# A layer's forward and backward in one kernel: split evictions, narrow tiles on demand, a sum over groups from two bf16 parts, a softmax gradient in halves

## The chip, the cores and the metric

One core of a Trainium2 chip runs the whole program. The time is that of one launch in device microseconds (us); lower is better. The engines are named as the profile names them: PE (matrix multiplication), PEld (its weight loads), DVE, ACT, POOL and SP. SP computes nothing here, it issues DMAs, and POOL and ACT can issue them too. Each engine runs its own list of instructions strictly in the order in which it was written.

## The reference

The program computes a layer's output and ten gradients. With `xn = layernorm(x)` (2048 tokens, 512 wide) the output is `x + A(xn) + B(xn)`.

A is attention with a recurrent memory, 32 heads of 128. The tokens are cut into 64 segments of 32. Segment `s` works on 40 rows: 8 memory rows and its own 32 tokens.

```
h = concat(mem, x_s)                       # 40 x 512
q, k, v = h Wq, h Wk, h Wv                 # 32 heads x 128
p = softmax(q k^T / sqrt(128) + mask);  o = (p v) Wo
mem, out_s = o[:8], o[8:]                  # mem goes to segment s+1
```

So segment `s+1` can't begin before `s` has given its memory: a chain of 64 steps forward, and in the backward pass a chain of 64 steps the other way, in which the gradient of the memory rows is handed from segment `s` to `s-1`. B is `relu(xn w1 + b1)^2 w2 + b2`, without a chain. In the code the eight rows of a segment that pass to the neighbour stand with its 24 other rows in the "A" tiles of 32 rows, and the remaining 8 rows of four segments are batched into "L" tiles of 32 rows, which are off the chain.

## The kernel before, in words

Four stages follow one another. (1) Layernorm and B, forward and backward. (2) The forward chain: 64 calls of `chain(s)`, with the batched work of 16 blocks of four segments (`l_proj`, `l_attn`, `blk_in`, `blk_out`) and two weight gradients of B (`dw_unit`, 14 units of 16 pairs of matmuls) as filler between the links. (3) The backward chain: another `chain(s)`, 64 steps, with `l_pre`, `l_post`, `load` and `blk_out`. (4) The weight gradients of A, dense 128x128 matmuls, with the gradient of the layernorm beside them.

In stages 1 to 3 the code does not issue instructions where it stands. Each piece of work is put into a `_Plan` as an operation with a cost for each engine that may run it, with the tiles that it reads and writes. `_Plan.run` then writes one order for all engines: it simulates them, ranks operations by the longest way to the end, adds a correction for each operation from the tables `BIAS_1` and `BIAS_2` and follows the parameters `PAR`. PSUM banks are handed out by the same planner (`Stage.bank`, with a limit for each kind). What the chip then does at its own pace keeps that order on every engine, so a late operand stops the engine that waits for it, and whatever stands behind.

PE runs three shapes of matmul: full tiles of 128x128 (plan form `f`: transposes, `blocks`, `dw_unit`), four column tiles of 128x32 side by side (`w`: `proj` at line 538, `dh_part` at L1370, `wo_part` at L1039, scores at L1161), and sixteen tiles of 32x32 of which the diagonal four are used (`d`: `diag` at L624, the second half of `mixed` at L599). Going from one shape to another is what the planner calls a turn. In the kernel before, each operation has one shape.

The forward step is `proj` of q and k (evicted by `evict`, 512 columns at once), transposes of both (`to_T`, L429), a mask matmul (L1153) and the scores into one PSUM bank (L1161), `weights` (row maximum L1007, subtraction L1008, exponential L1010), transposes of the weights on DVE (L1168, L1169), `diag` "o" (L624), whose result is scaled on eviction (L634 or L639), a DVE transpose (`sq_T`, L517), `wo_part` (L1039), and `mb` (L1046, L1047), from which matmul L1185 takes the memory rows that DVE copies (L1190) into the next segment's input `hA`. POOL normalises the weights for the backward pass (L1020, L1021).

The backward step is `proj` "gO" (L538), its transposes, `dP` into one PSUM bank (L1468), the softmax gradient `smax_bwd` (four DVE operations over all eight head groups, L1354 to L1359) giving `dS`, DVE transposes of it (L1501, L1502), and three parts 2, 1, 0 (gradients of v, q, k): each makes `dN` (L573, L588 with L599, L624), transposes it on DVE (L517) and multiplies with the weight into the bank `ps_dRA` (`dh_part`, L1370). Its sum `R_A` is evicted in float32 by two copies (ACT and DVE); 32 float32 matmuls with the selector `sel8` (L1524) sum it over the four groups of rows, and DVE copies the sum into `gT` of the next step (L1528), from which `proj` "gO" reads.

## Time and profile before

| | us |
|---|---|
| median of three runs | 2809.19 |
| lowest and highest run | 2799.02, 2809.37 |
| span of the profiled execution (first to last instruction) | 2798.3 |
| stage 1, from the start | 228 |
| stage 2, forward chain | 1007 |
| stage 3, backward chain | 1022 |
| stage 4, weight gradients | 542 |

No time of its own is given for the profiled execution beside its span. The stages are cut at the first matmul of the forward chain, the first of the backward chain, and where the weight gradients take over, so they overlap by a few us at the cuts. In the page, the busy time of PE counts from the start of a matmul to its modelled end, so that a single short matmul counts for its whole way through the array; how closely matmuls follow each other is better read from the starts in the timeline. A wait is named by the instruction that waited and the one that released it.

### The profile page before, as it was taken

How to read it: one execution, taken by the hardware profiler on the slowest of the kernel's cores; microseconds unless marked ns; L12 is line 12 of the kernel's file. 1: busy time of each engine (PE TensorE's matmuls, PEld its weight loads, DVE VectorE, ACT ScalarE, POOL GpSimd, SP SyncE). 2: the span in 40 equal slices, each digit the busy share in tenths (PEclk: the TensorE clock that was granted, in tenths of full speed). 3: DMA queues.
4: the chain of work that ended last, by engine and by line, in shares of the span. 5: the costliest groups of instructions: out<-in, count | busy, mean ns of one | idle time of the engine just before them, and what ended most of it. 6: DMA issues, size and time to landing. Idle time of an engine off the chain costs nothing.

```text
span 2798.3 us, 125071 instructions
## 1 busy us (share of the span) xinstructions
PE 2664.6 (95%) x54888; PEld 1538.5 (55%) x55072; DVE 1327.3 (47%) x3327; ACT 985.8 (35%) x2012; POOL 824.8 (29%) x2431
## 2 busy tenths in 40 slices
PE   8998999999999999999999999999999899999999
PEld 6664555555555555575555555555555444444444
DVE  5544455555455555565455455555455402232322
ACT  4333444444444444364444444444444300000000
POOL 1111111111111111145555555555555301112210
PEclk9999999999999999999999999999999999999999
DMA  6657656555557566647777676777766698788861
GB/s 211 202 172 205 180 160 175 164 166 163 156 169 186 169 185 175 177 118 178 187 181 187 179 189 179 189 192 190 188 182 177 201 344 273 232 255 270 257 185 42
DMA packets 499792, 530.91 MB, mean 190 GB/s; under 512 B 223845, under 2 KB 325398, under 8 KB 497070
## 3 DMA queue, kind: packets, MB, share of 16 engines
q1 hardware_dynamic: 480254, 463.06, 59.9%
q0 software_dynamic: 15056, 53.56, 5.6%
q8 instruction: 430, 7.05, 1.1%
q10 hardware_dynamic: 3936, 6.29, 0.7%
q14 instruction: 116, 0.95, 0.1%
HBM read 249.77 MB, written 237.52 MB: 174 GB/s over the span
## 4 chain that ended last, share of the span: by engine, by line
PE 45%; DVE 4%; issue 3%; DMA 3%; ACT 1%; POOL 1%; SPq 0%; DVEq 0%; ACTq 0%; POOLq 0%
PE ps_gw L1690 14%; PE ps_dRA L1370 8%; PE ps_gw L1694 5%; PE ps_gO L538 3%; PE ps_dRL L1370 3%; PE ps_d L624 2%; DMA dLN<-S_GNL 2%; PE ps_d L573 1%; PE ps_d L599 1%; PE ps_gOT L429 1%; PE ps_d L588 1%; PE ps_gm L1524 1%; PE ps_gL L538 1%; PE ps_dL L1481 1%; PE ps_dP L1468 1%
## 5 line engine op out<-in xcount | busy, mean ns | idle before, releaser
L1370 PE MATMUL ps_dRA<-WA,dT 128*32 128x512 bf16 x6144 | 377.0, 381 | 5.3 <-issue 2.5
L1690 PE MATMUL ps_gw<-WA,WB 128*128 128x512 bf16 x1505 | 330.6, 379 | 1.6
L1690 PEld LDWEIGHTS <-WB 128*128 128x128 bf16 x1896 | 185.4, 98 | 225.0 <-issue 1.7
L538 PEld LDWEIGHTS <-PA 128*32 128x32 bf16 x8192 | 195.4, 96 | 192.3 <-DVE PA L1190 22.3
L435 ACT CAST dN<-ps_d 128x512 bf16<-128x512 f32 x372 | 207.4, 590 | 184.7 <-PE ps_d L599 112.3
L1370 PEld LDWEIGHTS <-dT 128*32 128x32 bf16 x6144 | 151.8, 96 | 154.2 <-DVE dT L517 17.3
L433 DVE CAST gwo<-ps_gw 128x512 bf16<-128x512 f32 x64 | 40.0, 685 | 399.9 <-PE ps_gw L1690 268.5
L435 ACT CAST gwo<-ps_gw 128x512 bf16<-128x512 f32 x64 | 33.1, 598 | 510.2 <-PE ps_gw L1690 357.3
L517 DVE STREAM_TRANSPOSE dT<-dN 128x256 f32<-128x256 f32 x384 | 165.4, 437 | 72.1 <-ACT dN L435 66.5
L1020 POOL TENSOR_TENSOR P<-P,rsA 128x320 bf16<-128x320 bf16 x64 | 46.2, 722 | 458.8 <-DVE rsA L1015 244.1
L624 PEld LDWEIGHTS <-PB 32*32 32x32 bf16 x8192 | 119.8, 92 | 76.4 <-DVE PB L1168 23.9
L1701 POOL DMA_DIRECT2D out_dram<-gwo x96 | 71.6, 753 | 293.9 <-ACT gwo L435 265.1
L538 PE MATMUL ps_q<-WA,PA 128*32 128x512 bf16 x2048 | 145.2, 382 | 5.5 <-DVE PA L1190 3.7
L1039 PE MATMUL ps_RA<-WB,OT 128*32 128x256 bf16 x4096 | 129.0, 277 | 17.7 <-DVE OT L517 13.6
L538 PE MATMUL ps_k<-WA,PA 128*32 128x512 bf16 x2048 | 144.9, 381 | 0.3 <-DVE PA L1190 0.3
L435 ACT CAST kN<-ps_k 128x512 bf16<-128x512 f32 x125 | 73.4, 587 | 194.1 <-PE ps_k L538 172.2
L538 PE MATMUL ps_v<-WA,PA 128*32 128x512 bf16 x2048 | 140.7, 379 | 0.0
L1039 PEld LDWEIGHTS <-OT 128*32 128x32 bf16 x4096 | 103.9, 98 | 46.2 <-DVE OT L517 32.0
L538 PE MATMUL ps_gO<-WB,PA 128*32 128x512 bf16 x2048 | 126.4, 380 | 1.0 <-DVE PA L1528 1.0
L611 POOL COPY BDL<-bPLL 32x64 bf16<-32x64 bf16 x256 | 60.4, 236 | 218.4 <-PE ps_d L573 210.4
L433 DVE CAST qN<-ps_q 128x512 bf16<-128x512 f32 x62 | 42.9, 692 | 171.5 <-PE ps_q L538 169.5
L1254 PE MATMUL ps_dw<-sx,anT 128*128 128x512 bf16 x339 | 108.2, 384 | 6.6 <-DMA sx<-S_XN 2.8
(315 smaller groups left out, 5300.8 us busy)
## 6 DMA issues: line engine op xcount, KB each, us to landing
S_GN<-dN SPq DMA_DIRECT2D x192, 256.0 KB
WA<-S_GN SPq DMA_DIRECT2D x150, 256.0 KB
S_Q<-qN SPq DMA_DIRECT2D x64, 256.0 KB
S_K<-kN SPq DMA_DIRECT2D x64, 256.0 KB
S_V<-vN SPq DMA_DIRECT2D x64, 256.0 KB
S_ON<-oN SPq DMA_DIRECT2D x64, 256.0 KB
bqN<-S_Q SPq DMA_DIRECT2D x64, 256.0 KB
bkN<-S_K SPq DMA_DIRECT2D x64, 256.0 KB
```

The costliest lines, as they stand in the source:

```text
L433: nc.vector.tensor_copy(out, in_)
L435: nc.scalar.copy(out, in_)
L517: self.plan.add({"DVE": 0.445}, lambda e, half=half: nc.vector.transpose(words(dst, half).rearrange("p (i c r) -> p i c r", i=4, c=2), src ...
L538: nc.tensor.matmul(bk()[32 * j:32 * (j + 1), :], lhsT=win(dc), rhs=Wt(dc, c0), start=(dc == 0), stop=(dc == DC - 1), tile_position=(0, 32 ...
L611: f(q_(dst, j)[:, :, j, 0:c], q_(src_f(), j))
L624: nc.tensor.matmul(bk()[32 * j:32 * j + m, k * P:(k + 1) * P], lhsT=lf(j, i), rhs=rf(j, i), start=(k == 0 and x == 0), stop=(x == n - 1), ...
L1039: nc.tensor.matmul(bk()[32 * c:32 * (c + 1), :], lhsT=sg.rows(OTt, i, j), rhs=Wo[:, JQ * i + j, dh * DH:(dh + 1) * DH], start=(i == 0 and ...
L1254: nc.tensor.matmul(bks[x]()[:], lhsT=anT[x][:, c, :], rhs=sx[z][:], start=(c == 0), stop=(c == TC - 1))
L1370: nc.tensor.matmul(bk()[32 * j:32 * (j + 1), :], lhsT=sg.rows(XT, i, j), rhs=wtf(t, i, j), start=(first and i == 0), stop=(last and i == N ...
L1690: nc.tensor.matmul(bks[n](), lhsT=HNc[:, rc, dc * P:(dc + 1) * P], rhs=gns[y][:, hf * 512:(hf + 1) * 512], start=(y == 0), stop=(y == NRC ...
L1694: nc.tensor.matmul(bks[n](), lhsT=gns[y][:, k * P:(k + 1) * P], rhs=GOc[:, rc, :], start=(y == 0), stop=(y == NRC - 1))
L1701: nc.gpsimd.dma_start(outWs[t][dc * P:(dc + 1) * P, 4 * hf:4 * hf + 4, j, :], wt[:].rearrange("p (i e) -> p i e", i=4))
```

## The change

The edits lie in the planner and in stages 2 and 3; the work of stages 1 and 4 is as it was (two small mask tiles move into the pool of stage 1).

Planner: an operation can have two shapes (`"wf"`), and the planner takes the one that PE is in. A key can have parts. New costs, new `PAR`, and new tables `BIAS_1` and `BIAS_2` throughout, so that the order of both chains is a new one.

Forward: the evictions of q and k and of their transposes are cut in two (`evict2`); the scores lie in two banks of four head groups, and mask, maximum, subtraction, exponential and DVE transposes go by halves; the scaled eviction of "o" goes by quarters; `P40` has two buffers. `dw_unit` and the transposes off the chain may run as 128x32 tiles. The batched scores (and in the backward pass `dPL`) take one matmul with 64 columns where there were two with 32. `blk_out` moves only the 32 memory rows of a block, in both chains; the other rows of `S_HNA` and `S_GOA` are copied from DRAM to DRAM. These copies, the memory rows of K and V, and the rows for `dw_unit` (two blocks of rows to a DMA) are now issued by POOL instead of SP. The writer of the key `"tk"`, by which some copies were paced, is gone. The batched output rows go straight to the output, without `S_BL`, `S_OL` and the last copy.

Backward: `R_A` is read as two bf16 parts, its upper half words in place and `R_lo`, the rest, which DVE makes by a subtraction; 32 bf16 matmuls take the place of the 32 in float32. `dP` lies in two banks, and `smax_bwd` makes its four operations twice, on halves of four head groups.

```diff
-PAR = ((0.3, 0.3, 0.0), (0.61, 7.94, 4.04), (0.09, 2.05, 17.32))
+PAR = ((0.3, 0.3, 0.0), (0.0, 0.45, 38.57), (0.0, 0.41, 55.23))
...
-                turn = o.shape not in (None, shape)
+                turn = bool(o.shape) and shape not in o.shape
...
     def transpose_to(ps_ap, in_ap, base=0, form="f"):
         k = in_ap.shape[0]
+        if form == "w":
+            for c in range(4):
+                x = slice(32 * c, 32 * c + 32)
+                nc.tensor.transpose(ps_ap[x], in_ap[:, x], ident[:], tile_position=(0, 32 * c))
+            return
...
+    def copy_tokens(b, dst, src):
+        sg.dma(lambda: dst[b * P + RL:(b + 1) * P].rearrange("(r v) d -> r v d", v=SPB),
+               lambda: src[b * P:(b + 1) * P].rearrange("(v r) d -> r v d", r=SEG)[M:], [("tk", b * SPB - 2)], [], cost=0.7, eng="POOL")
...
+    SPLIT = ("q", "k")
+    SPLIT_T = ("qT", "kT")
...
+        def evict2(self, out_f, bk, in_f, key, prio, cost, n=2):
+            self.plan.parts[key] = [(key, x) for x in range(n)]
+            for x in range(n):
+                c = slice(512 // n * x, 512 // n * (x + 1))
+                self.plan.add(cost, lambda e, c=c: ev({"DVE": "v", "ACT": "s"}[e], out_f(c), in_f(c)), [bk], [(key, x)], prio)
...
         def to_T(self, kind, nm, src, skeys, out_f, okeys, prio):
+            form = "wf" if prio else "f"
...
-        sg = Stage(plan, pc, {"c": (5, F8), "f": (2, F8), "m": (2, F8), "t": (1, F8)})
+        sg = Stage(plan, pc, {"c": (6, F8), "f": (2, F8), "m": (2, F8), "t": (1, F8)})
...
+            for h in range(2):
+                x, bk = slice(4 * h, 4 * h + 4), bks[h]
+                A({"DVE": 0.325}, lambda e, x=x, bk=bk: V.tensor_reduce(mx[:, x], bk()[:], axis=AX.X, op=ALU.max), [bk], [("mxA", h)], 0)
+                A({"DVE": 0.325}, lambda e, x=x, bk=bk: V.tensor_tensor(
+                    out=st[:, x], in0=bk()[:], in1=mx[:, x].unsqueeze(2).to_broadcast([P, 4, KA]), op=ALU.subtract),
+                  [bk, ("mxA", h)], [("stA", h)], 0)
+                A({"ACT": 0.345}, lambda e, x=x: nc.scalar.activation(Et[:, x], st[:, x], ACT.Exp, scale=scale), [("stA", h)], [(pk, h)], 0)
...
             for nm, D_, S_ in (("S_V", S_VM, S_V), ("S_K", S_KM, S_K)):
                 sg.dma(lambda D_=D_: mrow(D_[b])[:, M * v:M * (v + 1), :], lambda S_=S_: mrow(S_[s])[:, 0:M, :],
-                       [(nm, s)], [(nm + "M", b, v)])
+                       [(nm, s)], [(nm + "M", b, v)], cost=0.7, eng="POOL")
...
-        sx = [tl("sx%d" % x, [P, D]) for x in range(5)]
+        sx = [tl("sx%d" % x, [P, 2, D]) for x in range(3)]
...
+                z = c // 2 % 3
+                if c % 2 == 0:
+                    sg.dma(lambda z=z: sx[z][:], lambda c=c: src[c * P:(c + 2) * P, :].rearrange("(c p) d -> p c d", p=P), [], [("sx", z)], lat=3.2, cost=0.62, eng="POOL")
 
                 def mm(e, c=c, z=z):
+                    w = 32 if e == "w" else P
                     for x in range(2):
-                        nc.tensor.matmul(bks[x]()[:], lhsT=anT[x][:, c, :], rhs=sx[z][:], start=(c == 0), stop=(c == TC - 1))
-                A(pe(0.435, "f", 2), mm, [("sx", z), ("anT", 0, c // HC), ("anT", 1, c // HC)], [bks[0], bks[1]])
+                        for m in range(0, P, w):
+                            nc.tensor.matmul(bks[x]()[m:m + w, :], lhsT=anT[x][:, c, m:m + w], rhs=sx[z][:, c % 2, :], start=(c == 0),
+                                             stop=(c == TC - 1), tile_position=(0, m))
+                A(pe(0.435, "wf", 2), mm, [("sx", z), ("anT", 0, c // HC), ("anT", 1, c // HC)], [bks[0], bks[1]])
...
+        R_hi = R_A.bitcast(BF16).rearrange("p (d z) -> p z d", z=2)[:, 1]
+        R_lo = tl("R_lo", [P, D])
+        sel8b = tl("sel8b", [P, M])
+        nc.vector.tensor_copy(sel8b[:], sel8[:])
...
+            for h in range(2 if sfx == "A" else 1):
+                x = slice(4 * h, 4 * h + 4) if sfx == "A" else slice(0, NI)
+                n = 4 if sfx == "A" else NI
+                c = cD if sfx == "L" else 0.315
...
                 for hf in range(2):
-                    def gm(e, hf=hf):
-                        for dc in (2 * hf, 2 * hf + 1):
-                            for j in range(JQ):
-                                nc.tensor.matmul(q_(bm(), j)[:, dc, :], lhsT=R_A[:, dc * P + 32 * j:dc * P + 32 * (j + 1)],
-                                                 rhs=sel8[:], start=(dc == 0), stop=True, tile_position=(0, 32 * j),
-                                                 skip_group_check=True)
-                    A(pe(0.31, "w", 16), gm, [("RA", hf)], [bm], 0)
+                    A({"DVE": 0.42}, lambda e, hf=hf: V.tensor_tensor(
+                        out=R_lo[:, 256 * hf:256 * hf + 256], in0=R_A[:, 256 * hf:256 * hf + 256], in1=R_hi[:, 256 * hf:256 * hf + 256],
+                        op=ALU.subtract), [("RA", hf)], [("Rl", hf)], 0)
+                for part_, key in ((R_hi, "RA"), (R_lo[:], "Rl")):
+                    for hf in range(2):
+                        def gm(e, hf=hf, part_=part_, key=key):
+                            for dc in (2 * hf, 2 * hf + 1):
+                                for j in range(JQ):
+                                    nc.tensor.matmul(q_(bm(), j)[:, dc, :], lhsT=part_[:, dc * P + 32 * j:dc * P + 32 * (j + 1)],
+                                                     rhs=sel8b[:], start=(dc == 0 and key == "RA"), stop=True, tile_position=(0, 32 * j),
+                                                     skip_group_check=True)
+                        A(pe(0.065, "w", 8), gm, [(key, hf)], [bm], 0)
...
-        sg.dma(lambda: seg_rows(out0flat, SEG, 0, M), lambda: seg_rows(S_OL, M, 0, M), [("gm", 0, SPB - 2)], [])
```

More of the change, by code (lines that the diff above doesn't have):

```diff
@@ L100, in pe @@
     x.shape = shape
-    x.n = n
+    x.n = {k: n * (4 if k == "w" and len(shape) > 1 else 1) for k in shape}
     return x
@@ L285, in run @@
                     elig.append(u)
-            seq.append((o, e))
+            seq.append((o, form if form and len(o.shape) > 1 else e))
         assert len(seq) == len(ops)
@@ L577, in blocks, with mixed @@
                            bk, lambda bk=bk: bk()[:], [(dst[0], half)], prio, EV_F)
-        def mixed(self, nm, pre, terms, rkeys, dst, prio, lift=0.0):
-            bks = [self.bank("d", [P, 512], F32, "ps_" + nm) for _ in range(2)]
-            for half in range(2):
+        def mixed(self, nm, pre, terms, rkeys, dst, prio, lift=0.0, full=False, inter=False, kind=None):
+            bks = [self.bank(kind or "d", [P, 512], F32, "ps_" + nm) for _ in range(2)]
+            for half in ((0, 1) if not inter else ()):
                 bk = bks[half]
@@ L699 @@
+        for i in range(NI):
+            nc.vector.tensor_copy(maskA[:, i, M:KA], mk[:])
         RB = 2 * P
@@ L1462, in chain @@
             sg.to_T_plain("c", "gOT", gN, "gN", gOT, "gOT", 0)
-            bk = sg.bank("c", [P, NI, KA], F32, "ps_dP")
+            bkp = [sg.bank("c", [P, NI // 2, KA], F32, "ps_dP") for _ in range(2)]
             for half in range(2):
```

361 lines of the change are left out of this document (194 added, 167 removed), and 55 rows, old and new, of tables (BIAS_1, BIAS_2).

## The prediction

> **What bounds the kernel now.** I read the totals first, then the stages, then what PE waited for in each chain, then single steps in order of time. The totals:
>
> ```profile
> span 2798.3 us, 125071 instructions
> PE 2664.6 (95%) x54888; PEld 1538.5 (55%) x55072; DVE 1327.3 (47%) x3327; ACT 985.8 (35%) x2012; POOL 824.8 (29%) x2431
> PEclk9999999999999999999999999999999999999999
> ```
>
> PE is busy for 95% of the span and the granted clock is full in all forty slices, so the time is the length of PE's list plus 134 us of gaps. The same by stage (columns: stretch, its length, then busy us and instructions of PE, PEld, DVE, ACT, POOL, then clock, DMA share, GB/s), with the rows that give the cuts:
>
> ```profile
> 228.00:1235.00 1007.00, 939.65 (x23959) 570.44 (x24066) 541.39 (x1316) 449.81 (x919) 154.95 (x294) 0.99 0.62 172
> 1235.00:2257.00 1022.00, 974.83 (x26969) 578.96 (x26969) 521.00 (x1291) 416.69 (x822) 540.22 (x1917) 1.00 0.72 186
> 2257.00:2799.00 542.00, 535.23 (x2442) 243.62 (x2490) 146.73 (x240) 33.15 (x64) 93.26 (x136) 1.00 0.73 228
> ...
> L538 PE MATMUL ps_q<-WA,PA x2048: 376/379/634, 228.5 to 1192.4; 128*32 128x512 bf16 x187
> ...
> L538 PE MATMUL ps_gO<-WB,PA x2048: 376/379/391, 1235.5 to 2211.5; 128*32 128x512 bf16 x187
> ...
> 2257.64 10.73 PE ps_gw L1690 x49
> ```
>
> The last stage, 542 us with 535 of PE, is dense and untouched; so is the first. What can move lies in the two chains: 67 us of PE gaps in the forward one, 47 in the backward one, and whatever a busy PE wastes. What PE waited for in the forward chain, then in the backward one (total, times, longest):
>
> ```profile
> PE ps_RA L1039 <- DVE OT L517: 13.6, 16, 2.0
> PE ps_o L624 <- DVE PB L1168: 10.2, 11, 4.1
> PE ps_mem L1185 <- DVE PB L1047: 7.4, 10, 1.1
> PE ps_q L538 <- DVE PA L1190: 3.7, 12, 0.3
> PE ps_dw L1254 <- DMA sx<-S_XN: 2.8, 4, 1.0
> ...
> PE ps_d L599 <- DVE maskA L1359: 3.4, 6, 1.2
> PE ps_gO L538 <- DVE PA L1528: 1.0, 3, 0.3
> ```
>
> The first four are links of the recurrence: 34.9 us in which the forward chain, not PE, set the pace. In the backward chain the link into the next step, `gO` on the copy L1528, costs 1.0 us in 63 steps: there PE has other work, and instructions removed from it count nearly in full.
>
> What a busy PE wastes shows in a forward step (start, duration; PE alone):
>
> ```profile
> 702.75 1.04 PE L1254 MATMUL ps_dw<-sx,anT 128*128 128x512 bf16 x3
> 703.86 0.22 PE L1185 MATMUL ps_mem<-sel,PB 128*32 128x16 bf16 x8
> 704.01 0.60 PE L1254 MATMUL ps_dw<-sx,anT 128*128 128x512 bf16 x2
> 704.55 0.61 PE L538 MATMUL ps_q<-WA,PA 128*32 128x512 bf16 x8
> ...
> 708.25 0.40 PE L429 MATMUL ps_qT<-ident,qN 128*128 128x128 bf16 x4
> ...
> 709.70 0.27 PE L1161 MATMUL ps_sc<-KT,qT 128*32 128x40 bf16 x16
> 709.81 0.60 PE L538 MATMUL ps_v<-WA,PA 128*32 128x512 bf16 x8
> ...
> 710.98 0.67 PE L1108 MATMUL ps_scL<-KT,qLT 128*32 128x32 bf16 x64
> 711.48 0.62 PE L538 MATMUL ps_v<-WA,PA 128*32 128x512 bf16 x8
> 712.03 0.39 PE L1254 MATMUL ps_dw<-sx,anT 128*128 128x512 bf16 x1
> 712.48 0.39 PE L429 MATMUL ps_hN<-ident,PA 128*128 128x128 bf16 x4
> 712.79 0.23 PE L624 MATMUL ps_o<-vN,PB 32*32 32x128 bf16 x4
> ```
>
> The 49 dense matmuls of 10.73 us above follow each other by 0.22 us. The two of `ps_dw` at 704.01 should so take 0.44 us, but the next shape starts 0.54 us after them: the turn costs 0.10. PE goes into full tiles four times in these ten us.
>
> And a backward step, around the hand-over and at a change of shape:
>
> ```profile
> 1560.62 0.37 ACT L435 COPY R_A<-ps_dRA 128x256 f32<-128x256 f32 x1 [2.98 <-issue]
> 1561.03 0.42 DVE L433 COPY R_A<-ps_dRA 128x256 f32<-128x256 f32 x1 [2.91 <-ACT R_A L435]
> 1561.23 0.59 PE L1524 MATMUL ps_gm<-sel,R_A 128*32 128x8 f32 x32
> 1561.75 0.23 PE L624 MATMUL ps_dqL<-bkLN,dSTLL 32*32 32x128 bf16 x4
> 1561.89 0.19 DVE L1528 CAST PA<-ps_gm 128x32 bf16<-128x32 f32 x1 [0.44 <-PE ps_gm L1524]
> 1562.31 1.91 PE L538 MATMUL ps_gO<-WB,PA 128*32 128x512 bf16 x32
> ...
> 1565.19 0.22 PE L573 MATMUL ps_d<-gON,BDP 128*128 128x128 bf16 x1
> 1565.25 0.22 PE L573 MATMUL ps_d<-gLN,BDL 128*128 128x128 bf16 x1
> 1565.40 0.23 PE L624 MATMUL ps_dqL<-bkLN,dSTLL 32*32 32x128 bf16 x4
> ```
>
> Full tiles of 128 columns follow by 0.06 us, and the next shape by 0.15: again 0.09 for the turn.
>
> **The sum, against the span of 2798.3 us.** The median of the three runs, 2809.19, lies 10.9 us above that span; I take the difference over.
>
> *Forward, turns.* With two shapes to choose from, `ps_dw` and `ps_hN` can stay in the narrow shape that PE is in. In the step shown the visits at 702.75 and 704.01 would each save two turns, that at 712.03 (between narrow and 32x32 tiles) one; the transposes of q and k at 708.25 keep theirs. Five turns of 0.10 us over 64 steps are 32 us; the low end is nothing, if the planner's new order does not use the choice. In narrow form the work of `ps_dw` itself is that of a projection, 8 matmuls in about 0.44 us (709.81 and its kind), so it is no dearer. Not each step holds as many visits: I take two thirds, -22.
>
> *Forward, waits.* The halves shorten the recurrence. A copy of 512 columns that becomes two of 256 on two engines:
>
> ```profile
> L435 ACT CAST dN<-ps_d 128x512 bf16<-128x512 f32 x372 | 207.4, 590 | 184.7 <-PE ps_d L599 112.3 <-PE ps_d L624 36.8 <-DVE gOT L433 9.8
> L1354 DVE TENSOR_TENSOR btA<-ps_dP,bP 128x320 f32<-128x320 f32 x64 | 31.3, 490 | 30.2 <-PE ps_dP L1468 29.3 <-DMA LT<-S_VM 0.6
> ```
>
> 0.59 us against 0.37 (the half copy of `R_A` on ACT): -0.2 at each of four places (q and k, their transposes, the scaled eviction, the start of the softmax on the first half of the scores), some 0.8 us a step. The turns take 0.34 us of cover from the same gaps (22/64), which leaves 0.46 against a mean wait of 34.9/64 = 0.55. Ends: none, and all 34.9; I take two thirds, -23. The extra instructions cost no time of their own while DVE and ACT are at 54% and 45% of the stage.
>
> *Small work on PE.* `ps_scL`, 64 matmuls in 0.50 us, becomes 32 twice as wide: between 0.25 and 0.50, so -0.2, 16 times; the same for `dPL`: -3 in each chain. The block transposes (712.48 to 712.79, less a turn: 0.2) become four narrow ones of 0.06: -0.15, 32 times, -2.5 in each chain.
>
> *Backward, the sum of R.* The 32 float32 matmuls take 0.52 us up to the next, 0.10 of it a turn. Sixteen narrow bf16 matmuls with 40 columns take 0.11 us (709.70 to 709.81), so 32 of them 0.22: -0.2 over 63 steps, -13. The strided read of the upper halves as weights has no row; if it doubled those 16, the gain would be -6, if the new ones cost as much as the old, 0. I take -13, by the nearest row. The page "TensorE: Matmul & The Clock Gate" of the Trainium skill, section "Back-to-back issue gap", speaks against this: it gives up to 64 columns a floor of some 60 cycles, 25 ns, for each matmul, by which 32 would take an estimated 0.8 us, +24 us instead of -13, and a sum of -24 instead of -61. The scores' row, 7 ns each over four column tiles, disagrees, so I leave that sum a place only within the second case below.
>
> *Backward, the link.* Before the lower part can be multiplied, DVE subtracts twice, each about as long as its copy of that width, 0.42. With ACT making both copies (done at 1560.99 and 1561.36), the subtractions end at 1561.83 and the copy L1528 starts near 2.05 instead of 1.89; with DVE making the second copy, near 2.5. So +0.15 to +0.6 us a step. In the step shown the copy ends 0.23 us before `gO` starts, because PE is on `ps_dqL`: that other work is the cover, and where it is used up the whole 0.15 to 0.6 counts, and the matmuls saved as well. Ends: 0 and 0.4 x 64 = 25; I take +8.
>
> *Backward, the halves of the softmax gradient.* From 0.42 at 256 columns and 0.49 at 320, 160 columns take 0.31: eight make 2.5 us where four made 2.0. The first half is done after 1.25, so part 1 can begin earlier; the DVE transposes of all `dS` come up to 0.5 later, less what the first `dP` bank is earlier. Ends: -5 (the wait at L599, 3.4, and some) and 0.2 x 64 = 13. I take 0, since what waits on `dS` now sums to a few us. DVE rises by some (0.5 + 0.84) x 64 = 86 us to 59% of the stage.
>
> *The moved DMAs.* Some 112 loads of `sx`, 128 copies of memory rows and 64 other copies go from SP to POOL. POOL's issues in this stage:
>
> ```profile
> L479 POOL DMA_DIRECT2D out_dram<-wt x28: 542/678/807, 319.6 to 1208.1; - x28
> ```
>
> At 0.68 us, 304 make 207 us, and POOL goes from 155 to 362 of 1007 us. I cost it at nothing while they are issued ahead of need; the price otherwise is the third case.
>
> Forward -22 - 23 - 5.5 = -50.5; backward -13 + 8 + 0 - 5.5 = -10.5; together -61. 2798.3 - 61 = 2737, and with 10.9: **2748 us**.
>
> **The rivals.** *The chains take it back* (0.24). The backward link costs its 25 and the halves their 13, against -18.5: +19.5, and with the forward gain -31, 2778. For it: PE's spare work shrinks in every step while the link grows. Against it: 1.0 us of waits there today.
>
> *Late loads from POOL, slower* (0.12). PE keeps its order, so each `sx` pair that lands late stops it in full. On POOL the load stands behind copies that must wait until K or V has landed in DRAM, and behind the normalisation L1020. Over 112 loads the break-even with -61 is 0.55 us each, and above 0.67 the kernel is slower by more than 0.5%; at 0.8 the time is 2809 - 61 + 90 = 2838. Against it: three buffers hold six blocks of rows where five were held, and today such waits are 2.8 us in all. The Trainium skill's "SBUF — State Buffer", section "Who interferes with whom", adds a reason: DVE in its two-port modes locks GpSimd out, descriptor generation with it. The spread of 542 to 807 ns in the row above agrees, but is at most 0.27 us an issue.
>
> *The change does not do what it says* (0.06). The new order seldom uses the second shape, and PE's saved work turns into waits: within 0.5%, about 2805.
>
> **How the numbers follow.** The sum has 0.58, with its own range 2700 to 2775: all turns and waits, and no cost of the link, give -32 - 35 - 11 - 13 = -91 and 2718, and an order that also closes other gaps some 20 less. About 0.5% (14 us) is what a measurement of this kernel tells from no change. Faster: 0.58 + 0.24 = 0.82; same 0.06; slower 0.12. The range 2690 to 2812 leaves out the late loads and about 0.05 below.
>
> **What would show it.** The forward stretch near 955 us and the backward near 1010; `ps_dw` largely as 128x32 tiles; the waits of `ps_RA`, `ps_o`, `ps_mem` and `ps_q` near 12 us together; `ps_gm` as 32 bf16 matmuls followed by the next within 0.3 us; the wait of `gO` on the copy of `ps_gm` under 10 us. I am wrong if PE waits on `sx` for tens of us, if `gO`'s wait grows past 20, or if the narrow form of `ps_dw` takes clearly more than 0.44 us a pair.

## The result, and the profile after

The changed kernel is slower. Its median is 2917.8 us of four runs (2912.8 to 2925.3) beside 2809.3 for the kernel before on the same chip: a ratio of 1.0395, 95% interval 1.0368 to 1.0422, some 108 us where I had forecast a gain of 61. The totals of the page, to be read against those of before:

```profile
span 2911.0 us, 130411 instructions
PE 2685.9 (92%) x56746; PEld 1544.9 (53%) x56746; DVE 1448.6 (50%) x4455; ACT 1001.0 (34%) x2287; POOL 1044.5 (36%) x2764
```

PE's busy time rose by 21 us and its gaps from 134 to 225. (More busy time isn't more work here: with the halves alone, below, nearly the same number of matmuls counts 15 us more.) By stage, cut at the first matmul of `ps_q`, the first of `ps_gO` and the start of the dense `ps_gw` (columns as in the prediction: stretch, length, busy us and instructions of PE, PEld, DVE, ACT, POOL, then clock, DMA share, GB/s):

```profile
231.00:1319.60 1088.60, 961.96 (x25910) 583.98 (x25906) 606.97 (x1996) 487.32 (x1250) 350.30 (x611) 0.98 0.61 160
1319.60:2360.60 1041.00, 959.05 (x26721) 566.59 (x26714) 575.88 (x1728) 392.12 (x759) 564.12 (x1932) 0.98 0.70 178
2360.60:2911.00 550.40, 546.94 (x2533) 247.73 (x2532) 146.66 (x240) 33.15 (x64) 93.83 (x137) 1.00 0.76 230
```

By the same cuts the chains of the kernel before take 1007.0 and 1012.4 us, so the forward chain lost 82 us and the backward chain 29. (The same forward chain takes 1089 to 1101 us in three profiles, of this kernel and of two runs that edit only the backward chain, so some 12 us in a single profile are chance.) In the forward chain PE's gaps went from 67 to 127 us. What PE waited for, in the forward chain and then in the backward one:

```profile
PE ps_RA L1089 <- DVE OT L536: 25.5, 48, 1.5
PE ps_o L669 <- issue: 12.2, 9, 3.1
PE ps_vL L563 <- POOL PB L1111: 11.1, 1, 11.1
PE ps_mem L1238 <- DVE PB L1097: 9.0, 18, 1.0
PE ps_kT L435 <- DVE kN L439: 8.9, 5, 3.8
...
PE ps_dP L1536 <- DVE gOT L439: 36.9, 13, 6.5
PE ps_d L643 <- DVE maskA L1429: 11.6, 25, 0.8
```

Forward, the waits that I had put at 12 us together have grown: `ps_RA` alone from 13.6 to 25.5. Beside them stands a kind without a releaser, "issue", inside groups that had begun: 29 us in all where it was 7. The single wait of 11.1 us is of another kind, and I come back to it under "Instructions that come late". Backward, a wait that was 0.8 us before, `dP` on the copy of `gOT`, is now 37. Whether the halves did what I priced shows in one forward step (start, duration; ACT and DVE on the evictions):

```profile
716.90 0.41 ACT L441 CAST qN<-ps_q 128x256 bf16<-128x256 f32 x1
717.13 0.41 DVE L439 CAST kN<-ps_k 128x256 bf16<-128x256 f32 x1
717.47 0.41 DVE L439 CAST qN<-ps_q 128x256 bf16<-128x256 f32 x1
...
718.04 0.29 DVE L439 COPY KT<-ps_kT 128x256 bf16<-128x256 bf16 x1 [0.16 <-PE ps_kT L435]
...
718.36 0.37 ACT L441 COPY KT<-ps_kT 128x256 bf16<-128x256 bf16 x1 [1.05 <-DVE KT L439]
...
724.59 0.42 DVE L682 TENSOR_TENSOR oN<-ps_o,rsA 128x256 bf16<-128x256 f32 x1 [1.19 <-PE ps_o L669]
725.04 0.63 ACT L687 ACTIVATE oN<-ps_o,rsA 128x128 bf16<-128x128 f32 x2 [2.10 <-DVE oN L682]
```

The second half of a bank begins when the first has ended, at all three places. At the transpose and at `o` the releaser named is the other engine's copy; at `q` DVE came straight from its half of `k`. Half and half take 0.29 + 0.37 us for a transpose that DVE copied whole in 0.42. Over all steps (counted from the trace, medians), the stretch from the projections of q and k to the scores grew by 0.25 us at their eviction and by 0.56 at that of the transposes, and the scaled eviction of `o` by 0.38; the halves of the scores and of the softmax saved 0.83 of 2.37. That is +0.36 us a step in all, where I had -0.2 at each of four places. The hand-over of a backward step:

```profile
1559.48 0.42 DVE L439 COPY R_A<-ps_dRA 128x256 f32<-128x256 f32 x1 [0.80 <-ACT R_A L441]
1559.82 0.79 DVE L1589 TENSOR_TENSOR R_lo<-R_A 128x256 bf16<-128x256 f32 x2
1560.66 0.21 PE L1597 MATMUL ps_gm<-sel8b,R_lo 128*32 128x8 bf16 x8 [0.16 <-DVE R_lo L1589]
1560.94 0.19 DVE L1601 CAST PA<-ps_gm 128x32 bf16<-128x32 f32 x1 [0.33 <-PE ps_gm L1597]
```

From the end of the last copy of `R_A` (1559.90) to the start of the copy into `gT` it takes 1.04 us; before it took 0.44.

### The profile page after: what moved, and what is told of

Its sections match the earlier page's. It is cut to its first block, busy times and chain, and to the rows that moved or that the text cites. A ratio compares the mean times of both kernels' runs of the same rounds, so it can differ in the third digit from the quotient of the medians.

```text
span 2911.0 us, 130411 instructions
## 1 busy us (share of the span) xinstructions
PE 2685.9 (92%) x56746; PEld 1544.9 (53%) x56746; DVE 1448.6 (50%) x4455; ACT 1001.0 (34%) x2287; POOL 1044.5 (36%) x2764
## 4 chain that ended last, share of the span: by engine, by line
PE 39%; DMA 4%; DVE 3%; issue 3%; SPq 1%; ACT 1%; POOL 0%; ACTq 0%; POOLq 0%
PE ps_gw L1764 14%; PE ps_dRA L1440 7%; PE ps_gw L1768 5%; PE ps_gO L563 3%; DMA dLN<-S_GNL 2%; PE ps_d L669 2%; PE ps_dRL L1440 2%; PE ps_d L606 1%; PE ps_d L643 1%; PE ps_gOT L435 1%; PE ps_dP L1536 1%; PE ps_dL L1549 1%; SPq L498 1%; DVE R_lo L1589 1%; PE ps_d L621 1%
## 5 line engine op out<-in xcount | busy, mean ns | idle before, releaser
L563 PEld LDWEIGHTS <-PA 128*32 128x32 bf16 x8192 | 195.3, 96 | 180.2 <-issue 15.2
L498 POOL DMA_DIRECT2D S_KM<-S_K x64 | 34.0, 531 | 369.0 <-DMA S_K<-kN 304.2
L1089 PE MATMUL ps_RA<-WB,OT 128*32 128x256 bf16 x4096 | 136.3, 275 | 30.5 <-DVE OT L536 25.5
L656 POOL COPY BDP<-bP 32x256 bf16<-32x256 bf16 x256 | 102.6, 401 | 129.8 <-PE ps_d L606 82.2
L563 PE MATMUL ps_k<-WA,PA 128*32 128x512 bf16 x2048 | 134.5, 380 | 5.9 <-DVE PA L1243 5.1
L563 PE MATMUL ps_q<-WA,PA 128*32 128x512 bf16 x2048 | 137.7, 379 | 1.8 <-issue 1.8
L1310 PE MATMUL ps_dw<-sx,anT 128*32 128x512 bf16 (+1 forms) x1750 | 124.1, 383 | 5.1 <-issue 3.4
L439 DVE CAST kN<-ps_k 128x256 bf16<-128x256 f32 x128 | 54.2, 424 | 120.2 <-ACT kN L441 105.6
L656 POOL COPY BSLK<-dSL 32x64 bf16<-32x64 bf16 x256 | 60.4, 236 | 139.7 <-PE ps_dL L1549 130.5
```

What stands on the lines that cost most here:

```text
L439: nc.vector.tensor_copy(out, in_)
L563: nc.tensor.matmul(bk()[32 * j:32 * (j + 1), :], lhsT=win(dc), rhs=Wt(dc, c0), start=(dc == 0), stop=(dc == DC - 1), tile_position=(0, 32 ...
L656: f(q_(dst, j)[:, :, j, 0:c], q_(src_f(), j))
L1089: nc.tensor.matmul(bk()[32 * c:32 * (c + 1), :], lhsT=sg.rows(OTt, i, j), rhs=Wo[:, JQ * i + j, dh * DH:(dh + 1) * DH], start=(i == 0 and ...
L1310: nc.tensor.matmul(bks[x]()[m:m + w, :], lhsT=anT[x][:, c, m:m + w], rhs=sx[z][:, c % 2, :], start=(c == 0), stop=(c == TC - 1), tile_posi ...
```

## The experiments

Where a comparison needs it, ratios are to the kernel before on the same chip; an edit to the changed kernel compares with 1.0395, and 0.001 of a ratio is 2.8 us. "Same order" means that every engine's list keeps its sequence.

**Two engines at one bank.** A small program of its own: sixteen times each, PE fills a bank and ACT and DVE copy half of it each, into one tile (`one`), into two tiles (`sep`), by halves of the partitions (`quad`), or from two banks (`two`).

```diff
+ mm(b); S.copy(d[:, 0:256], b[:, 0:256]); V.tensor_copy(d[:, 256:512], b[:, 256:512])   # one
+ mm(b); mm(c); S.copy(d[:, 0:256], b[:, 0:256]); V.tensor_copy(d[:, 256:512], c[:, 256:512])   # two
```

> The disputed cost by itself; the layer's whole work is left out. One matmul fills a bank, then ACT copies one half of it and DVE the other, sixteen times for each case: both into one tile (ps_one), into two tiles (ps_sep), from two banks into one tile (ps_two), from two sets of 64 partitions of one bank (ps_quad), and the whole bank by ACT or DVE alone (ps_allA, ps_allV). Theory 1, one bank serves one engine at a time: in ps_one and ps_sep DVE starts when ACT's copy of 0.37 us has ended, so the pair takes about 0.8 us where the whole takes 0.59 (ACT) or 0.69 (DVE); in ps_two both start together and the pair ends after 0.42. Theory 2, it is the common destination: ps_one is serial, ps_sep runs side by side, ps_two is serial. ps_quad is open under both.

Its waits (total, times, longest; in the other eight of sixteen DVE was busy until then), and its groups with busy us and mean ns:

```profile
DVE oneA L38 <- ACT oneA L37: 6.5, 8, 2.0
DVE sepB L43 <- ACT sepA L42: 5.2, 8, 0.6
DVE quad L54 <- ACT quad L53: 4.7, 8, 0.7
DVE two L49 <- PE ps_two L29: 2.4, 5, 0.7
```

```profile
L62 DVE CAST allV<-ps_allV 128x512 bf16<-128x512 f32 x16 | 10.5, 692 | 10.5 <-PE ps_allV L29 10.1
L58 ACT CAST allA<-ps_allA 128x512 bf16<-128x512 f32 x16 | 9.4, 585 | 1.4 <-PE ps_allA L29 0.8
L38 DVE CAST oneA<-ps_one 128x256 bf16<-128x256 f32 x16 | 6.8, 425 | 6.6 <-ACT oneA L37 6.5
L37 ACT CAST oneA<-ps_one 128x256 bf16<-128x256 f32 x16 | 6.0, 372 | 6.9 <-PE ps_one L29 6.4
```

From one bank DVE waits for ACT wherever it is free, whatever it writes to, and starts some 0.03 us after ACT has ended; from two banks it waits only for PE, and in eleven of sixteen it runs beside ACT. So two halves take 0.37 + 0.42 = 0.80 us where one engine needs 0.59 or 0.69. The wait is a semaphore in the program; the trace does not say what the banks would do without it. The Trainium skill's "PSUM — Partial Sum Buffer", section "PSUM bank collisions raise a hardware error", says that two engines at one bank and the same 32 partitions at a time are an error, two readers included, and that different quadrants are allowed. `quad`, with 64 partitions for each engine, was kept apart all the same, so no run here shows what that would give.

**The halves alone, in the kernel before.** The evictions of q, k, their transposes and `o` are cut in two there, in the same order.

```diff
+ ev("s", o[:, :n], i[:, :n])
+ ev("v", o[:, n:], i[:, n:])
```

> The kernel before with its order kept; only the evictions of q, k, their transposes and the scaled eviction of o are cut in two, one half on ACT and the other on DVE. The prediction's step (a half takes 0.37 to 0.42 us where the whole took 0.59 to 0.69, so 0.2 us less at each place): forward chain 10 to 25 us shorter. The theory from the run of single copies (two engines' copies from one bank follow one another, so a place takes the sum of both halves): 0.25 us more at q and k, 0.5 at the transposes, 0.4 at o, about 1.1 us a step, 40 to 75 us longer in 64 steps.

1.0137 (1.0122 to 1.0152). Its forward chain, and PE's longest wait in it:

```profile
229.80:1271.80 1042.00, 955.10 (x23965) 566.91 (x24075) 601.63 (x1608) 506.65 (x1266) 154.88 (x294) 0.99 0.59 167
...
PE ps_RA L1048 <- DVE OT L517: 39.7, 73, 2.5
```

35 us longer than before's 1007.0, with the same matmuls on PE: a little under the range for serial copies, and the opposite sign of my step. The wait behind the cut eviction of `o` was 13.6 us before; 26 of the 35 us stand there.

**The halves taken out of the changed kernel.** Whole evictions of the same five, same order.

```diff
- ev({"DVE": "v", "ACT": "s"}[e], out_f(c), in_f(c))
+ x + 1 < n or ev(by, out_f(slice(0, 512)), in_f(slice(0, 512)))
```

> The changed kernel with its order of work on every engine, but the two halves of each eviction of q, k, their transposes and o made by one copy of the whole bank, at the place of the second half (ACT for q, k and the transpose of q, DVE for the transpose of k and for o). Theory 1, halves of one bank run one after the other and so lengthen the recurrence: the eviction of q and k shrinks from 0.9 to 0.7 us, that of the transposes from 1.0 to 0.6, that of o from 1.6 to 1.2, a forward step by about 0.8 us, the forward chain from 1088 to about 1040 us, the kernel by about 50 us. Theory 3, the new order of work is what costs: the forward chain stays within 15 us of 1088.

1.0307 (1.0267 to 1.0347): 25 us back, and the forward chain takes 1063.5. The wait behind `o`, 25.5 us with the halves, is now

```profile
PE ps_RA L1089 <- DVE OT L536: 10.8, 26, 1.2
```

The link, counted from the first projection of a step to the first matmul of `ps_mem`, fell from 14.8 to 14.1 us in the median step, under the 14.4 of the kernel before, but the mean step only from 16.3 to 15.9, where before's is 15.2. So the halves are a cause, and not the only one.

**POOL's queue.** POOL's waits in the changed kernel begin with K, and V follows, until they have landed in DRAM:

```profile
POOL S_KM L498 <- DMA S_K<-kN: 304.2, 52, 10.7
...
POOL S_VM L498 <- DMA S_V<-vN: 63.1, 30, 5.1
```

Same order, these copies issued by SP:

```diff
- [(nm, s)], [(nm + "M", b, v)], cost=0.7, eng="POOL")
+ [(nm, s)], [(nm + "M", b, v)], cost=0.7, eng="POOL", via="SP")
```

> After's code and order, but the eight-row copies of K and V (S_KM, S_VM) are issued by SP, as before, and no longer by POOL. Theory A (POOL's list is blocked by them: POOL stood 304 us at S_KM and 63 us at S_VM in after): the forward chain gets 30 us or more shorter, to about 1055. Theory B (TensorE waits for its instructions: queue 8, which brings 16 KB = 128 matmuls at a time, falls behind while the sx pairs that POOL issues run beside the anT transposes; 35 stalls of 36 us in the forward chain end 1.25 to 1.6 us after such a packet, in before 13 of 9 us): these copies are small, so the forward chain stays within 12 us of after's 1088 and the stalls stay at 30 us or more.

1.0392 (1.0337 to 1.0446): nothing. These waits of 300 us held up nobody.

**Instructions that come late.** What led to this one is a stretch of the changed kernel in which PE stands inside a group that has all its operands (timeline of PE; then the DMA queues from 434.1 to 441.0 us, and from 441.0 to 442.2, with packets, MB and share of 16 engines; then the stretch behind the stall, with the granted clock third from the end):

```profile
439.91 0.22 PE L669 MATMUL ps_o<-vN,PB 32*32 32x128 bf16 x4
439.97 0.22 PE L669 MATMUL ps_o<-vLN,PB 32*32 32x128 bf16 x2
443.33 0.23 PE L669 MATMUL ps_o<-vLN,PB 32*32 32x128 bf16 x2 [3.15 <-issue]
```

```profile
q1 hardware_dynamic: 1379, 0.78, 74.3%
q0 software_dynamic: 138, 0.41, 26.2%
```

```profile
q1 hardware_dynamic: 536, 0.16, 196.2%
q14 instruction: 1, 0.01, 8.6%
q8 instruction: 1, 0.02, 5.5%
```

```profile
443.33:446.80 3.47, 3.47 (x60) 1.63 (x62) 2.80 (x7) 0.59 (x1) 1.26 (x3) 0.56 0.70 226
```

Queue 8 brings instructions in packets of 16 KB. In the first stretch none comes, while transposes of `anT` (SP) and pairs of `sx` (POOL) fill the DMA engines; the second has one, and some 1.3 us after its end PE goes on, for the next 3.5 us at little over half clock. Such stalls lie 128 matmuls apart, or a multiple of it (from 894 to 916 us: 128, 128, 256 records; the 24 gaps without a releaser in this chain all do, with at most two records missing), so a packet holds 128 matmuls with their weight loads. I counted all gaps of over 0.25 us that end 1.25 to 1.62 us after the end of a packet (without the chain's first 21 us and its last 5). Some 3 us of each figure are chance: so much lies in most other windows of this width after a packet.

```
kernel                                  forward us   stalls at packets: number, us
before                                    1007.0        13     9.0
changed                                   1088.6        35    35.7
changed, whole evictions                  1063.5        33    45.7
changed, K and V copies on SP             1098.7        37    36.6
changed, sx on SP                         1054.4        22    18.8
changed, sx and copies on SP              1074.9        24    22.8
before, narrow tiles                      1006.0        27    16.7
before, sx on POOL                         996.9        10     9.7
changed, three parts undone               1031.3        19    16.2
the same with full tiles                  1048.6         9     9.5
```

Same order, the pairs issued by SP, behind the transposes:

```diff
- [], [("sx", z)], lat=3.2, cost=0.62, eng="POOL")
+ [], [("sx", z)], lat=3.2, cost=0.62, eng="POOL", via="SP")
```

> After's code and order, but the sx pairs are issued by SP, behind the anT transposes, and no longer by POOL beside them. Theory B (instructions come late while both run): no interval of more than 9 us between instruction packets during the transposes, stalls that end at such a packet fall from 36 us to under 18, fewer half-clock stretches behind them, the forward chain 20 to 40 us shorter, total about 2885. Theory A (POOL's list blocked by the K and V copies): under 10 us. Rival C (the delay comes from the transposes alone, whatever runs beside): stalls and total as in after, within 10 us, or slower because the pairs now come late on SP.

1.032 (1.0277 to 1.0364), 21 us less, and the stalls halved, 17 us of the 21:

```profile
230.10:1284.50 1054.40, 956.48 (x25914) 580.03 (x25910) 606.79 (x1996) 487.98 (x1250) 264.44 (x492) 0.99 0.59 165
```

The longest interval between two packets fell from 11.0 to 8.9 us (apart from one of 14 us at the end of the chain, which both have). Another 4 us is the single wait above, `ps_vL` on POOL's copy into `PB`: that copy starts at 249.90 us, behind three pairs of `sx` and seven copies of `S_GOL` that POOL has issued since 240.35. With the pairs on SP it starts at 244.88 and the wait is 7.0 us; in the kernel before the copy ran at 242.81 and PE did not wait for it. With both kinds of transfer on SP:

> After's code and order with both, the sx pairs and the copies of K and V on SP. Theory A and theory B together give the sum of the two runs before; if SP's queue is the limit (two DMAs of 0.3 to 0.5 us a step more on it), less than the better of the two.

1.032 (1.0274 to 1.0367): by the time, the pairs are all of it. (The forward chain of this profile is 20 us longer than that of the run before, 1074.9, and the backward chain 12 us shorter; 21 us of waits for the memory rows `VM`, 6 in the run before, stand in it.)

**The same transfers, in the kernel before.** Its `sx` loads, one block of rows each, issued by POOL, same order.

> The kernel before with its order kept; only the sx loads are issued by POOL instead of SP (one block of rows to a DMA, as before). If loads on POOL's queue beside the anT transposes are what delays TensorE's instructions: stalls that end at an instruction packet rise from 9 us to 18 or more in the forward chain, which gets 10 to 40 us longer. If the narrow tiles alone make the stalls of after: within 8 us of before.

0.9979 (0.9962 to 0.9995): stalls of 9.7 us as against 9.0, and 6 us faster, the one version here that beats both kernels, by little. So loads on POOL do not delay instructions by themselves. What differs in the changed kernel is that the narrow tiles make PE use up its packets faster (next run) and that a pair is twice as large; the two were not told apart. Long intervals between packets are not new either: the kernel before has four of 8.7 to 10 us.

**The narrow tiles alone.** In the kernel before, same order; `dw_unit` and the transposes off the chain take 128x32 tiles where PE stands in that shape.

```diff
+ form[o.idx] = now = now if now in "wf" else (nxt if nxt in "wf" else "f")
```

> The kernel before with its order, its engines and its DMAs kept; only the matmuls of dw_unit and the transposes off the chain are cut into 128x32 tiles where TensorE stands in that shape. This is the one part of the change that I priced highest (turns saved in the forward chain, 22 us, two thirds of the turns at 0.10 us). Theory of the prediction: forward chain 10 to 20 us shorter, total about 2795. Rival D (four times the instructions for the same work, and their supply is near its limit: 128 matmuls in a packet, packets at least 3.5 us apart): the stalls at instruction packets rise from 9 us by 5 to 20 and take the gain back, total within 8 us of before or above it.

1.0037 (1.0019 to 1.0054), 10 us slower. The turns of the forward chain fall from 555 to 332, and the chain stays as long (1006.0): its stalls at packets are 8 us more, so that without them it would be 9 us shorter, a difference and not a measurement. The backward chain, where the transposes are cut too, is 16 us longer with stalls of 27 us instead of 15. In the changed kernel's order, with halves, `sx` and sum undone, the way back to full tiles:

```diff
-                o.fn(e)
+                o.fn("f" if e == "w" else e)
```

> The three parts undone together (whole evictions, sx on SP, float32 sum), and in the same order the matmuls of dw_unit and the transposes off the chain are always full 128x128 tiles. If saved turns are a gain once TensorE is not held up elsewhere (the prediction's 0.10 us a turn): some 200 turns more in the forward chain, 10 to 25 us longer, total 2855 to 2870. If the narrow form gives back what it saves (as in before's order, where 222 turns fewer left the forward chain as long): within 8 us of 2843. If its instructions cost more than its turns: below 2835.

1.0208 (1.0182 to 1.0235) against 1.0148 for the same kernel with narrow tiles: 17 us slower over both chains. In the forward chain there are 284 turns more and 7 us of stalls less; the two profiles, which lie further apart than the medians, show 17 us there and 9 in the backward chain. So the saved turns are a gain in the order that was made for them, and none in before's.

**The sum of R.** The float32 sum put back, same order; the two subtractions and the second 16 matmuls fall away.

```diff
- lhsT=part_[:, dc * P + 32 * j:dc * P + 32 * (j + 1)], rhs=sel8b[:]
+ lhsT=R_A[:, dc * P + 32 * j:dc * P + 32 * (j + 1)], rhs=sel8[:]
```

> The changed kernel with the sum of R over groups as before: 32 float32 matmuls at the place of the first bf16 part, no subtraction, nothing at the place of the second; the order of everything else is the same. If the link sets the pace, R_A to the end of the sum falls from about 0.95 to 0.4-0.6 us and the backward stretch from 1050 to about 1025 us. If PE's other work covers the link, the shorter link and the longer matmuls cancel and it stays within 8 us of 1050.

1.0329 (1.0285 to 1.0373), 19 us less, of which the backward chain shows 14 (1027.3). Counted in the median, the step from the last copy of `R_A` to the end of `gm` is 0.42 us in float32 and 0.67 + 0.27 in two bf16 parts. And PE is not relieved: from the start of each of these matmuls to the start of PE's next it is 21 us over the 63 steps in float32 and 40 in bf16, with the waits for `R_lo` in it. Without gaps of over 0.1 us the 32 take 0.26 us in float32 and 0.22 in bf16.

**The late copies of gOT.** In one step of four, DVE stands at the transposes of `dLN` (88 us in all) with the copies of `gOT` behind it. First the load was made independent of the writes just before it, by reading a buffer that was finished long ago in its place:

```diff
- sg.dma(lambda: flat(dLN), lambda t=t: part_of(S_GNL[t], b, BPC),
+ sg.dma(lambda: flat(dLN), lambda t=t: part_of(S_ONL, b, BPC),
```

> The changed kernel with one load of the backward chain replaced: dLN in l_post is read from rows that were finished long before (S_ONL) instead of from the gradient rows just written, so the gradient of the batched memory rows is left out of the result and nothing waits for those writes; the order of work is the same. Theory 4, DVE stands at the transposes of dLN until the load has landed, and the copies of gOT queued behind them hold up dP: PE's 37 us of waits in front of dP go, and the backward stretch falls from 1050 to about 1018 us. Theory 5, the backward loss is the longer link and the halved softmax: it stays within 10 us of 1050.

1.038 (1.035 to 1.0411); DVE still waits 80 us. The backward chain of the profile is 13 us shorter and PE's wait at `dP` 25 us, but the run with the float32 sum, which left these loads alone, has 27 there: the writes are not most of it. Then without the loads (the gradients of the batched rows are not made):

```diff
- sg.dma(lambda: flat(dLN), lambda t=t: part_of(S_GNL[t], b, BPC),
+ plan.add({"SP": T_DMA}, lambda e: None,
```

> After without the loads of dLN in l_post (the transposes LT read what l_pre left in the tile, so the gradients of the batched rows are not computed). If the late landing of dLN, for which DVE stood 88 us with the copies of gOT queued behind, is what lengthens one backward step in four: TensorE's wait at dP for gOT falls from 37 us to under 10, the long steps from 17 to 23 us to at most 17, the backward chain by 15 to 30 us to about 1018. If those steps are long because of the work that lies in them: under 8 us.

1.0262 (1.0247 to 1.0278), the backward chain 1002.4, the wait for `gOT` gone: 39 us of that chain as an upper bound. Before that was tried in full, three parts were undone together:

> After's order with three parts undone together: whole evictions, sx loads on SP, the sum of R in float32. If the three causes are separate, the gains add (alone 20, 25 and 12 us): total about 2860, forward chain about 1030, backward about 1027. If they hide one another: 2875 or more.

1.0148 (1.0132 to 1.0164). Alone the three gave 25, 21 and 19 us, by their intervals each to within some 14; together 69, to within 9. So they add, and some 40 us are left. On top of this the loads of `dLN` went into tiles of their own and up to 8 us earlier in SP's list, with nothing left out:

```diff
+ while seq[k - 1][0].end > o.end - 8.0 and seq[k - 1][0] not in hard:
+     k -= 1
```

> The three parts undone together as in the run before it (whole evictions, sx on SP, float32 sum), and the loads of dLN go into two tiles of their own, so that SP may issue each up to 8 us earlier; nothing is left out. If the late landing of dLN costs what the run without its loads gave back (39 us in the backward chain) because of the place of its issue: DVE's wait for dLN falls from some 85 us to under 40, the backward chain from 1027 to about 1000, total about 2815. If SP's queue is full and the loads land no earlier: within 8 us of 2843.

1.0149 (1.0118 to 1.018): nothing, although the wait is gone. The waits for `dLN` and at `dP` without the earlier loads, then what stands with them:

```profile
DVE LT L536 <- DMA dLN<-S_GNL: 95.4, 30, 9.0
PE ps_dP L1536 <- DVE gOT L439: 38.7, 13, 6.5
PE ps_d L643 <- DMA bqN<-S_Q: 1.5, 2, 0.8
```

```profile
DVE LT L544 <- DMA dLX<-S_GNL: 24.9, 13, 4.4
PE ps_d L651 <- DMA bqN<-S_Q: 17.2, 12, 3.2
PE ps_dRA L1449 <- DVE dT L544: 7.8, 7, 2.2
PE ps_gO L571 <- issue: 7.6, 8, 2.3
```

DVE's wait falls by 70 us and PE's by 39, and other waits take its place: 16 us more for `q`, whose loads SP issues too, and the rest spread over `dT`, gaps without a releaser and POOL's `maskL`. That the loads moved ahead pushed back those of `q` fits this and was not tested. The 39 us come back when the 48 loads of 256 KB are not made, and not when they are made earlier.

**A mixture.** Forward chain of the kernel before with `sx` on POOL, backward chain of the changed kernel with the float32 sum and the earlier loads.

> A mixture: the forward chain of the kernel before (order, whole evictions, whole softmax, full-width dw_unit) with sx issued by POOL, and the backward chain of the changed kernel (its order, the softmax gradient in halves) with the sum in float32 and the earlier dLN loads. If the stages are separate and what was found holds: forward 997 to 1007, backward 990 to 1010, total 2760 to 2790, faster than both. If the forward chain of before needs its own backward stage (transfers that spill over the border), or the dLN loads land no earlier: backward about 1027, total about 2810.

1.0062 (1.004 to 1.0083), slower than before and as the second case has it; forward 1008.4, backward 1030.6 beside before's 1007.0 and 1012.4. The backward part is the dearer one even behind the other forward chain, and POOL's `sx` bring the forward chain nothing here.

## Why the prediction was wrong, point by point

Against the forecast of -61 us the change cost 108. Undoing the cut evictions, the pairs of `sx` on POOL and the bf16 sum gives 69 of them back; some 40 stay.

*What bounds the kernel.* That PE is busy most of the time held (92%). That instructions removed from its list count nearly in full did not follow from it: the gaps, which I let only shrink, grew by 91 us. PE's busy time, which I read as the length of its list, grew as well, although the list has fewer turns.

*Forward, waits (-23).* This step failed, in its sign. I took the duration of a half copy, 0.37 us, as the time of a cut copy, which needs both halves to run at once. The halves of one bank follow one another: 0.80 us for a pair of single copies, 0.66 at a transpose. Alone it costs 35 to 38 us in the kernel before, and taking it out of the changed one gives 25. The prediction itself quotes a row that says so, the second copy of `R_A` with `ACT R_A` as its releaser; I read its duration and not its bracket. The fourth of my places, the softmax, did gain: its halves lie in two banks.

*Forward, turns (-22).* The mechanism was right in the order that was made for it: -17 over both chains, some 365 turns in the forward one where there were 555, and a pair in narrow form no dearer (0.43 us in both). It missed that four times the matmuls use up instruction packets faster: in before's order the stalls grew by 20 us in both chains, and the kernel was 10 us slower.

*The moved DMAs (nothing).* This failed too, but not as my rival had it. PE waited for `sx` less than 2 us in all; moving the copies of K and V back gave nothing; but the pairs on POOL cost 21 us, some 17 by holding up PE's own instructions beside the transposes and 4 by standing before POOL's copy into `PB`.

*The sum of R (-13) and the link (+8).* Both terms were mis-sized; together they cost 19 us (the chain alone 14) where I had -5. The 0.52 us that I read as the price of the float32 matmuls hold a wait: in the rows that I quoted they begin at 1561.23 and the second copy of `R_A` ends at 1561.45. The kernel before has 62 such gaps in its 63 steps, 0.25 us each in the mean. Without it they take 0.28 us against 0.22 in bf16, 3 to 4 us in all instead of 13. The link, from the last copy of `R_A` to the copy into `gT`, grew from 0.44 to 1.00 us in the median step, the upper end of my 0.15 to 0.6; I counted 8 of the 36 us that this makes in 64 steps. The page "TensorE: Matmul & The Clock Gate" of the Trainium skill, section "Back-to-back issue gap", whose floor I weighed, was not the reason: without waits the 32 in bf16 start 4 ns apart in the median, where the floor has 25. Of my rivals, "the chains take it back" had this link at its full price, but left the forward gain standing.

*The halves of the softmax gradient (0).* Counted in the median, the step to `dS` fell from 2.38 to 1.86 us, and the median backward step from 15.3 to 15.0, or 14.7 with the float32 sum. The chain is not shorter for it: PE is busy for 959 of its 1041 us, and the steps at the end of a block take mostly 17 to 23. What I had as nothing in the sum shows as nothing in the time; that the next limit takes the gain is likely, but the halves were not undone by themselves.

*The wait of gO (under 10 us)* held, 0.6 on the copy of `ps_gm`; the wait arose one link further, at `dP`, 37 us, which no rival named.

*What stays open.* With three parts undone the forward chain is still 24 us longer than before's, although its link is shorter in the median (14.1 us against 14.4) and narrow tiles gain. Its steps by place in a block are 14.4, 13.9, 15.6 and 18.2 us long, before's 15.1, 14.9, 15.3 and 15.4. Its longest wait is new:

```profile
PE ps_oL L669 <- DMA VM<-S_VM: 15.6, 8, 3.3
```

Once in a block PE stands for the batched memory rows of V; that was 2.0 us in the kernel before and 1.0 in the changed one, and it is 16 to 21 us in all three versions of this kernel and in that with both kinds of transfer on SP. That PE, held up less elsewhere, now comes before them is likely and was not tested. Half clock is another part: 41 us of that chain where before has 20, which at half speed is at most 10 us more (an estimate). Whether the order itself is at fault, which was made with costs in which halves run side by side, was not tested by itself. Nor is the backward chain's remaining 15 us explained, nor small work on PE (-5.5 a chain) told apart.

## What to carry to other kernels

Before an eviction is cut in two for two engines, look in the trace for two engines reading one bank: if the second's releaser is the first, as here, a cut costs the sum of the halves, and only halves in two banks gained. A step that makes matmuls smaller also makes more of them for the same work; count the instruction packets and what else is on the DMA engines. Before matmuls get a price from the distance to the next instruction, look whether an operand landed in between. And with PE busy nearly all the time, a wait taken off one queue came back at another here: loads made earlier gave nothing, loads not made gave 39 us.

## What the runs showed of the hardware

Instruction supply was a limit that I had not thought of, although the planner has it (`_LINE = 128`, `_FETCH = 4.2` us). A packet of 16 KB came 3.3 to 3.4 us after the one before at the fastest and 4.9 to 5.2 in the median of the forward chain; under the `anT` transposes the interval grew to 9 to 12 us, and PE went on 1.3 to 1.6 us after a packet had landed. The Trainium skill's "Runtime: NRT & Kernel Launch", section "Instruction fetch mechanics", has the 16 KB and 256 instructions, which the distances of 128 matmuls agree with, and says that the fetch is mostly hidden. In these runs it was not: 36 us of the changed kernel's forward chain stand at packets.

A gap can cost twice. The granted clock stood at half for 20 us of the forward chain before and for 28 to 61 in three profiles with the changed one's forward chain, in stretches of 3.4 us or a multiple, nearly all at or behind a gap of PE, also behind gaps of 2 us. In the stretch shown above four matmuls of 512 columns side by side follow the four before by 0.43 us, where it is 0.22 at full clock.

For these tiny tiles float32 is hardly dearer than bf16: the 32 matmuls of 8 columns start 6 to 7 ns apart in float32 and 4 ns in bf16, in the median.
